# A long convolution's second stage split by halves of the channels, with a new written-out order

## The chip, the core and the metric

The kernel runs on one core of a Trainium2 chip. The metric is the device time of one execution in microseconds. The core has a matrix engine (TensorE, PE in the profile; PEld is its weight load), a vector engine (VectorE, DVE), a scalar engine (ScalarE, ACT), GpSimd (POOL), and SyncE (SP), which here only issues DMA transfers. Each engine works through its own queue in order; engines wait for one another on semaphores.

## What is computed

The input is a sequence of 2048 positions with 640 channels. A modulation vector from `c` and `w_mod` gives six vectors (sa, ca, ga, sb, cb, gb). The first half of the block is a long convolution, the second an MLP that shifts groups of channels along the sequence:

```python
mod = (_silu(c) @ w_mod).reshape(c.shape[0], 6, 1, -1)
h = _layernorm(x) * (1 + ca) + sa
# A: k_shift = four-tap convolution of k; kv = k_shift * v
kv_f, kf_f = rfft(kv padded to 4096), rfft(ssm_k padded to 4096)
y = irfft(kv_f * kf_f)[:2048] + kv * ssm_D
x = x + ga * (h * y)
h = _layernorm(x) * (1 + cb) + sb
# B: h1 = gelu(layernorm(h) @ w1), groups of it shifted by +-1, +-2; x1 = h + h1 @ w2
x = x + gb * (x1 + gelu(layernorm(x1) @ w3) @ w4)
```

## The kernel before

**The work.** The transforms are written as matrix products in two stages each, over 640 channels in five blocks (b0 to b4) of 128. The filter `ssm_k` (called s; `ssm_D` is added to its first column, L461) and kv go through the same forward transform:

- `to_slots` (L395): a 32x32 transpose on DVE for each block, 2048 columns.
- `stage1` (L408): for each block, half h of the positions inside it and quarter, four matmuls into PSUM, evacuated (L208 on ACT, L210 on DVE) as 128x1024 into `T01`, whose two halves `T0` and `T1` are the two values of h. One h holds 160 of the 320 values that the second stage has on its free axis.
- second stage: for each of 32 frequencies k, products of the table `Gs` (in `RG`) with `T01`, evacuated into `KSX` (buffer `R3`) for s and `XS` (buffer `R5`) for kv. For s this is `stage2` (L416): one frequency at a time over both halves, four matmuls of 320 columns and one evacuation of 128x640. For kv it is `stage2_half` (L434): one half at a time, three frequencies together, twelve matmuls of 160 columns and one evacuation of 128x960 (of 128x640 for the last two frequencies).

`inverse1` (L624 to L650) multiplies the spectra on DVE (L633, two products of 128x2048 for each of ten pieces, the second with a copy of s's piece whose partition halves are swapped by two DMAs, L629, into one of four buffers KSY), does the first inverse stage on PE (L644, L645) and evacuates into `T01`. `inverse2` (L673, L685) does the second. `k_shift` (L472) is the four-tap convolution on PE (L480) and the product with v on DVE (L485). Then for groups of tiles come `chain_a`, `chain_b`, `chain_c` (layer norms on DVE, ACT and POOL), `mm_w1`, `mm_w2`, `mm_w3`, `mm_w4`.

**Loads.** SP issues s's blocks (L229), the transposing loads of k and v (L234, one per block), copies that complete the table `Gs` (L354, L355), the input x (L540, in two sets of four), the twelve half loads of `w_mod` (L503; six early ones into `RH` and `RK`, six later ones into `R3`; each is used by five matmuls, L509), sixteen copies `RH<-RK` (L592), the KSY copies (L629) and the loads of w1 (L661), w2 (L662, L664), w3 and w4 (L1020 to L1023). POOL issues some of the copies.

**The order.** All work is added as numbered tasks. `ORDER` lists every task once: number, engine letter (P, A, D, G for POOL, S for SP) and for a PSUM tile its place, one of four. Each engine performs its tasks in the order of the list. The costs in `add` were used by the planner that wrote the list; at run time they do nothing.

Of the kernel before, what the change touches and what calls it, by code (L numbers as in the profile page):

```python
# [26 lines left out]
0S 2S 19G 18D 21G 20D 27G 29D 23D 4S 50G 28D 24A 36G 37G 22D 30A 68G 69D 25A 26G 88P:0 31A 89A 86P:1 87A 56G 90P:2 91A 72G 84P:3 5S 85A 3S 38G 39G 40A  # L27
73D 104P:0 106P:1 107A 70D 6S 49G 71D 105D 98P:2 102P:3 103A 99A 8S 118P:0 74G 94P:1 95A 75D 114P:3 115A 108P:2 109A 9S 119D 112P:0 113A 1S 66D 116P:1
41G 42G 43G 67D 80P:3 81A 117D 51D 52D 110P:2 44A 45D 10S 111D 96P:0 97A 82P:1 122P:3 11S 123D 32G 34G 54A 33S 53A 83A 76P:0 77A 100P:2 101D 92P:1 93A
78P:3 7S 120P:0 46G 136D 79A 55G 121D 175P:2 176A 47S 195P:1 196A 35S 179P:3 180A 185P:2 186D 147P:1 141P:0 193P:3 142D 148A 57G 58G 181P:2 182D 59G  # L30
139P:1 194A 140A 201S 199P:0 48S 200A 143P:3 144D 155P:2 165P:1 166D 156A 161P:0 162A 202S 191P:3 192D 12S 157P:2 158A 167P:1 168D 13S 163P:0 164A
197P:3 198A 145P:2 203S 146D 189P:1 65G 151P:0 152D 169P:3 190A 204S 183P:2 170A 184D 159P:1 160A 177P:0 178D 153P:3 154A 173P:2 174A 149P:1 150D
137P:0 260P:3 254D 171P:2 187P:1 138A 60A 188A 61G 62G 63G 261A 214D 172A 14S 124P:0 266P:1 210D 267A 125D 126P:3 127D 15S 211D 255D 209A 258P:2 259A
16S 270P:1 271A 130P:0 131D 268P:3 64A 262P:2 343G 269A 263A 215A 128P:1 264P:3 129D 256D 276P:2 277A 265A 134P:0 132P:1 17S 135D 282P:2 212A 283A
133D 216G 286P:3 223S 224P:0 220S 213G 278P:1 287D 225A 226S 279A 232S 284P:2 257D 221P:0 229S 285A 272P:3 227P:1 222A 228D 274P:2 235S 275D 273A
290P:0 291A 469D 288P:1 289A 233P:3 234D 292P:2 293A 294P:0 296P:3 230P:1 297A 298P:2 295D 299A 466D 342S 253G 246S 248G 312P:0 308P:3 309A 231D 463D
300P:1 301A 313D 460D 251G 310P:2 311D 367G 243S 306P:0 307A 316P:3 317D 280P:1 281A 252G 314P:2 304P:0 302P:3 305A 249S 240G 315D 236P:1 303A 237D
318P:2 319D 467D 340P:0 345D 241S 341A 338P:1 339A 238S 242G 326P:3 327A 344D 245S 250G 366S 322P:2 334P:0 352D 330P:1 331D 323A 244G 335A 239G 247G
324P:3 325A 346P:2 350S 351G 353D 347A 348P:0 360D 320P:3 349A 321A 328P:1 329A 354P:2 355A 359G 358S 361D 374S 356P:0 368D 369D 332P:3 333A 375G
362P:1 363A 364P:2 376D 365A 336P:3 337A 370P:1 371A 357A 372P:2 377D 378P:3 379A 380P:1 381A 383G 382S 385D 384D 386P:0 390S 391G 392D 393D 398S 373A  # L40
388P:3 387A 217A 399G 401D 394P:1 400D 425S 396P:2 397A 408D 407G 389A 402P:0 406S 409D 404P:2 395A 414S 416D 405A 415G 417D 464D 465D 426P:3 403A
427D 452S 410P:1 411A 412P:2 413A 420P:0 421D 418P:1 419A 422S 423P:3 456S 461D 470D 424D 468D 462D 218A 475P:20 477D 476A 520D 459G 454S 499D 500D
471D 521D 472A 540D 434S 219G 523D 541D 543D 437S 438P:1 439A 512A 435P:3 428S 429P:2 430A 431S 432P:0 501A 522A 433A 436A 525D 502G 504D 457S 478P:12
480A 503G 524G 526D 505D 473D 491P:03 545D 542A 544G 507D 553A 492A 527A 474D 546D 479A 571D 568D 485P:20 528G 529G 493A 530D 531P:1 506A 508G 509D
510P:3 486A 208S 547A 487A 458G 511A 548D 549G 481G 569D 570A 572D 573A 482P:20 484A 550D 551P:3 552A 532D 536P:1 533A 513D 537A 207S 574D 483D 575G
576D 580D 577D 517P:0 518A 581D 582D 583A 538P:3 578D 584G 579A 539A 585G 488P:21 489A 556P:0 557A 534D 535D 558P:3 559A 515P:2 516A 453S 514D 631D
632D 633A 586D 589D 590P:0 587P:3 455S 560P:2 634D 206S 635D 637G 591D 636A 638G 554D 561D 563D 588A 639D 562A 600P:0 601A 598P:3 599A 643D 640D 641D
642A 564G 494S 565D 644D 645D 646A 205S 441A 647D 490A 648G 566P:2 498G 567D 444D 651D 555D 605P:0 606D 607A 602P:3 649D 443D 603D 497S 652S 650S 699D
700D 447D 604A 620P:2 621A 495S 616P:1 617A 618P:0 661P:3 619A 662A 659P:2 660A 622P:1 623A 608D 609G 440D 610D 611P:0 613D 614P:3 615D 701A 663P:2
666P:1 664D 612A 683P:3 665A 667D 668A 681P:0 682A 677P:2 445G 656A 653D 654D 442G 655D 592D 669D 670G 674A 678A 671D 672P:1 673D 679P:0 680A 675P:1  # L50
593D 594D 702D 703D 496S 624P:2 595D 596D 676A 519G 597D 765D 749P:0 704A 705G 706G 766D 767A 768D 684A 707A 449A 625D 711D 747P:1 685P:32 712D 748A
769D 713D 714A 708D 709D 715D 771G 626D 446D 770A 710A 745P:1 716G 686P 717A 718S 772G 450D 719D 687D 720S 729P:3 773D 448G 750A 629S 774D 775D 777A
778D 779D 746A 727P:0 721D 781D 722D 723D 834D 835D 780A 776A 730A 627S 451G 790A 787A 657D 658D 782G 783D 743P:1 785D 791D 728A 731P:3 831D 832D 630S
688D 833A 732D 744A 733A 734P:0 735D 784S 786S 793P:1 794A 795P:3 737D 693D 694D 697S 736A 751P:02 796A 797P:1 800P:3 752P 738G 741D 836A 837G 838G
839D 753D 840D 798D 692S 739A 740S 742S 815P:0 843D 844D 801D 803D 841D 696S 813P:1 811P:3 845D 847G 842A 846A 848G 851D 788D 816A 849D 724A 725D 689S
809P:0 799A 852S 802A 804G 807D 814A 810A 812A 805D 850S 853P:1 759D 854A 808S 855P:2 856A 806S 875P:0 876A 869P:3 857P:1 873P:2 871P:0 726D 792D 874A
690S 789D 628S 754D 691S 891D 892D 894D 870A 860P:2 760D 951D 872A 895D 896A 695S 817P:30 893A 897G 898G 952D 954D 861D 862A 858D 863D 877P:21 953A
818P 903A 758S 904D 819D 899D 900D 698S 820D 859A 864G 865A 955G 905D 866S 906A 879D 822S 878P 867A 868S 933P:3 824S 901D 907G 902A 908G 909D 934A
911D 910S 956D 957D 958D 825D 912S 915P:2 935P:0 936A 913P:3 916A 763S 931P:0 757S 959A 914A 917P:2 929P:3 932A 960G 930A 961G 756S 821S 823S 962D
755S 963S 966P:0 967A 918D 919A 826D 885D 886D 920P:2 921D 830S 888S 829S 923G 762S 764S 922A 964P:1 965A 937P:30 969P:2 761S 880D 924G 968G 970D  # L60
972P:1 1003P:2 939D 925A 881S 1004D 926S 973D 975G 927A 928S 987P:3 988A 983P:2 971A 981P:1 890S 984A 1006G 974A 1005A 883S 889S 882S 827S 982A 985P:3
828S 976G 977D 1007G 938P 945D 979A 1008A 978S 980S 1010P:2 1011A 1012P:1 884S 1009S 946D 949S 1016P:0 1017A 948S 940D 942S 944S 1014P:2 943S 986A
989P:03 887S 1013A 1036P:1 991D 992D 996S 994S 1038P:0 990P 1015A 947S 997D 1034P:2 1039A 941S 1018P:03 1035A 1032P:2 1033A 998D 999S 1001S 993S 1002S
1042D 1043D 1000S 950S 1020D 1021D 1025S 1024S 1022S 1023S 1019P 1026D 1037A 995S 1027D 1031S 1029S 1030S 1028S 1040P:02 1044D 1045D 1047S 1046S 1048S
1049S 1041P 1050D 1051D 1052S 1053A 1054S 1055A
"""


# [69 lines left out]
def kernel(  # L138
# [4 lines left out]
    nc = tc.nc  # L143
# [11 lines left out]
    add = pl.add  # L155
# [444 lines left out]
    for h in range(2):  # L600
        stage2_half(h)
# [487 lines left out]
```

## Time and profile before

| what | value |
|---|---|
| median of 5 runs | 305.42 us (304.51 to 308.19) |
| the profiled execution | 308.19 us, its span 306.3 us, mean granted clock 0.965 |
| PE busy | 271.5 us (89%), 3054 matmuls |
| DVE, ACT, POOL busy | 218.1 us (71%), 210.2 us (69%), 112.2 us (37%) |
| stage 1, PE (L408) | 160 matmuls, 22.3 us |
| second stage of s, PE (L425) | 128 matmuls of 64x320, 11.2 us |
| second stage of kv, PE (L446) | 256 matmuls of 64x160, 10.4 us |
| evacuations of s's second stage | 20 on ACT (728 ns), 12 on DVE (819 ns) |
| products of spectra, DVE (L633) | 20, of some 1.22 us each |

The span runs from the first instruction to the last. Busy time counts what an engine's instructions cover; overlapping instructions make a busy PE no proof of a PE at its peak. "Idle before" in a group's line is the time in which the engine stood just before it, with what ended that wait.

### The profile page before, as it was taken

The page shows a single profiled execution, that of the slowest core. Times are in us where ns is not written, and L with a number is a line of the kernel's source. Part 1 is how long each engine was busy: PE and PEld are TensorE (multiplying, and loading weights), DVE is VectorE, ACT ScalarE, POOL GpSimd, SP SyncE. Part 2 cuts the span into 40 slices and gives each one's busy share as a digit, 9 for nine tenths or more (in the row PEclk, how much of TensorE's full clock was granted, in tenths as well). Part 3 has the DMA queues.
Part 4 walks back from the last instruction along what each step waited for, and adds up shares of the span by engine and source line. Part 5 has one row for each costly group of instructions (what it writes and reads, how often), then busy time and mean ns, then how long its engine had stood idle before and what let it go on. Part 6 is the DMA issues. An engine that isn't in the chain of part 4 may idle for free.

```text
span 306.3 us, 7652 instructions
## 1 busy us (share of the span) xinstructions
PE 271.5 (89%) x3054; PEld 207.1 (68%) x3054; DVE 218.1 (71%) x432; ACT 210.2 (69%) x352; POOL 112.2 (37%) x251
## 2 busy tenths in 40 slices
PE   0899999999889458687999989999999999999993
PEld 0655655777787236566887777688867886887771
DVE  8998999999899978869769986656475064031442
ACT  4789999999999699886768776276561752814110
POOL 4968553362104765341525660230152121400000
PEclk9999999999999855899999999999999999999999
DMA  6999999999899920642800112223004123130111
GB/s 216 261 191 202 221 205 162 262 234 209 202 226 303 244 49 2 204 144 46 288 3 1 24 39 55 54 43 77 2 18 86 28 55 70 26 86 5 32 51 43
DMA packets 58115, 35.75 MB, mean 117 GB/s; under 512 B 39872, under 2 KB 54848, under 8 KB 58080
## 3 DMA queue, kind: packets, MB, share of 16 engines
q1 hardware_dynamic: 56768, 31.55, 44.0%
q0 software_dynamic: 1216, 3.67, 4.9%
q8 instruction: 24, 0.39, 0.6%
q14 instruction: 11, 0.09, 0.1%
q10 hardware_dynamic: 96, 0.04, 0.1%
HBM read 16.31 MB, written 2.62 MB: 62 GB/s over the span
## 4 chain that ended last, share of the span: by engine, by line
PE 47%; DMA 15%; DVE 11%; SPq 7%; POOL 7%; issue 6%; ACT 6%; DVEq 0%; ACTq 0%; POOLq 0%
PE ps_w L931 17%; PE ps_w L961 15%; SPq L234 5%; PE ps_w L842 4%; PE ps_w L897 4%; DVE Rb L633 3%; DMA R<-in_A_v_dram 3%; DMA RG<-in_B_w_dram 3%; ACT RG L753 2%; POOL lnv L739 2%; DMA R<-RK 2%; DMA RH<-in_w_mod_dram 1%; DMA R<-in_w_mod_dram 1%; DMA RK<-R 1%; DVE Rb L395 1%
## 5 line engine op out<-in xcount | busy, mean ns | idle before, releaser
L931 PE MATMUL ps_w<-R,T 128*128 128x256 bf16 (+1 forms) x630 | 64.6, 261 | 1.1 <-DMA R<-RH 0.6
L931 PEld LDWEIGHTS <-T 128*128 128x128 bf16 x630 | 55.7, 98 | 8.7 <-issue 2.6
L935 ACT ACTIVATE R<-ps_w 128x1024 bf16<-128x1024 f32 (+2 forms) x36 | 29.0, 829 | 47.1 <-PE ps_w L931 47.0
L961 PE MATMUL ps_w<-T,R 128*128 128x320 bf16 x416 | 59.0, 299 | 0.0
L961 PEld LDWEIGHTS <-R 128*128 128x128 bf16 x416 | 40.2, 98 | 15.6 <-issue 0.5
L208 ACT CAST T<-ps_s 128x1024 bf16<-128x1024 f32 x34 | 32.7, 1027 | 3.6 <-PE ps_s L408 3.6
L753 ACT ACTIVATE RG<-R 128x640 bf16<-128x640 bf16 x32 | 23.6, 736 | 13.4 <-DVE R L780 9.0
L408 PE MATMUL ps_s<-F1bd,Rb 128*128 128x256 bf16 x160 | 22.3, 290 | 9.1 <-DVE Rb L395 8.8
L984 DVE TENSOR_TENSOR T<-ps_w,R 128x640 bf16<-128x640 f32 x15 | 12.3, 822 | 22.2 <-PE ps_w L952 11.5
L208 ACT CAST R<-ps_s 128x640 bf16<-128x640 f32 (+1 forms) x36 | 27.4, 845 | 0.9 <-PE ps_s L425 0.6
L408 PEld LDWEIGHTS <-Rb 128*128 128x128 bf16 x160 | 16.3, 104 | 15.1 <-DVE Rb L395 9.6
L897 PE MATMUL ps_w<-RG,R 128*128 128x320 bf16 x160 | 23.5, 300 | 0.0
L739 POOL TENSOR_TENSOR lnv<-lnv,mhalf 128x2 f32<-128x2 f32 (+1 forms) x29 | 22.5, 777 | 2.3
L842 PE MATMUL ps_w<-R,RG 128*128 128x256 bf16 (+1 forms) x200 | 21.2, 269 | 1.1 <-ACT Rb L208 0.5
L726 POOL TENSOR_SCALAR lnv<-stat 128x2 f32<-128x2 f32 (+1 forms) x14 | 5.4, 386 | 44.3 <-DVE Ra L764 17.2
L842 PEld LDWEIGHTS <-RG 128*128 128x128 bf16 x200 | 18.2, 108 | 3.3 <-issue 1.8
L904 DVE SCALAR_TENSOR_TENSOR R<-ps_w,R 128x640 bf16<-128x640 f32 x16 | 12.9, 819 | 10.6 <-PE ps_w L897 10.6
L644 PE MATMUL ps_i<-EA,Rb 128*128 128x128 bf16 x160 | 19.2, 219 | 1.0 <-DVE Rb L633 0.8
L645 PE MATMUL ps_i<-EB,Rb 128*128 128x128 bf16 x160 | 19.0, 219 | 1.3 <-DVE Rb L633 1.3
L897 PEld LDWEIGHTS <-R 128*128 128x128 bf16 x160 | 15.4, 98 | 6.1 <-issue 0.5
L480 PE MATMUL ps_ksh<-R,RQ 128*128 128x512 bf16 x80 | 18.8, 380 | 0.4 <-POOL RQ L356 0.4
L208 ACT CAST T<-ps_i 128x1024 bf16<-128x1024 f32 x19 | 18.2, 1046 | 0.9 <-PE ps_i L645 0.8
(179 smaller groups left out, 523.1 us busy)
## 6 DMA issues: line engine op xcount, KB each, us to landing
Ra<-in_A_ssm_k_dram SPq DMA_DIRECT2D x5, 512.0 KB, 5.1
Ra<-in_A_q_dram SPq DMA_DIRECT2D x8, 320.0 KB, 7.2
R<-in_w_mod_dram SPq DMA_DIRECT2D x6, 400.0 KB, 7.3
out_dram<-RH SPq DMA_DIRECT2D x60, 40.0 KB, 1.6
T<-in_B_w_dram SPq DMA_DIRECT2D x1, 2160.0 KB, 9.8
T<-in_B_w_dram SPq DMA_DIRECT2D x1, 2080.0 KB, 9.8
RH<-in_w_mod_dram SPq DMA_DIRECT2D x4, 400.0 KB, 5.9
RK<-R SPq DMA_DIRECT2D x5, 256.0 KB, 4.0
```

Source lines behind the costliest of these rows:

```text
L208: nc.scalar.copy(dst, src(ps.tile))
L408: nc.tensor.matmul(psv[:, ml, :], lhsT=xL[:, s0:s0 + P], rhs=F1r, start=True, stop=True)
L480: nc.tensor.matmul(pt[:, i, :], lhsT=diagw[:, b, jj, :], rhs=kT[:, b, c0:c0 + 512], start=(jj == 0), stop=(jj == 3))
L644: nc.tensor.matmul(psv[:, w, :], lhsT=Av[:, r_, :, g_], rhs=EAf, start=True, stop=False)
L645: nc.tensor.matmul(psv[:, w, :], lhsT=Bv[:, r_, :, g_], rhs=EBf, start=False, stop=True)
L739: nc.gpsimd.tensor_tensor(rs, rs, mhalf[:, 0:n], ALU.pow)
L753: add("ACT", 0.74, lambda e: nc.scalar.activation(junk, src, ACT.Square, scale=float(D) ** -0.5, accum_out=stat[:, li, 1, t:t + 1]), r=[sk ...
L842: nc.tensor.matmul(pt[:, fb, 0:cw], lhsT=w1_sb[:, b, 160 * fb:160 * fb + P], rhs=hT[:, b, 0:cw], start=(b == 0), stop=(b == ND - 1))
L897: nc.tensor.matmul(pt[:, hf, 0:320], lhsT=gsf[:, fb, c0:c0 + P], rhs=w2_sb[:, fb, 320 * hf:320 * hf + 320], start=(fb == 0), stop=(fb == 4))
L931: nc.tensor.matmul(pt[:, fl, 0:cw], lhsT=w3_sb[:, b, fb * P:(fb + 1) * P], rhs=xT[:, b, 0:cw], start=(b == 0), stop=(b == ND - 1))
L935: nc.scalar.activation(g3[g % 2][:, f0:f0 + fn, 0:cw], ps.tile[:, 0:fn, 0:cw], ACT.Gelu_apprx_tanh)
L961: nc.tensor.matmul(bank(i, hf), lhsT=gg[:, fb, i * P:(i + 1) * P], rhs=w4_sb[:, fb, 320 * hf:320 * hf + 320], start=(fb == 0 and i == 0), ...
```

## The change

Three edits. The function `stage2` goes; `stage2_half` takes the destination and its buffer as arguments and is called for s as well as for kv, so s too is done by halves of the channels, in threes of frequencies: 22 PE tasks and 22 evacuations in place of 32 and 32. The planner's cost of a PE task in it goes from 0.17 to 0.145 per frequency. `ORDER` is written anew for the 1036 tasks there now are (1056 before); task numbers above the second stage of s are lower by 20.

```diff
-    def stage2(XSd, dreg):
-        for k in range(32):
-            ps = Slot()
...
-                psv = pst(ps, name="ps_s2")[:, :, 0:320].rearrange("p g (h s) -> p g h s", h=2)
...
-    def stage2_half(h):
+    def stage2_half(XSd, dreg, h):
         for k0 in range(0, 32, 3):
             kn = min(3, 32 - k0)
...
-            t0 = add("PE", 0.17 * kn, f, r=[("T01", 10240 * h, 10240 * h + 10240), ("RG", 192 * k0, 192 * (k0 + kn))], alloc=ps, ni=8 * kn)
-            w = [("R5", 10240 * h, 10240 * h + 10240, "s2"), ("kT", 4 * h, 5, "s2")] + ([("vT", 0, 5, "s2")] if h else [("kTp", 0, 1, "s2")])
-            t1 = evac(XS[:, 160 * h:160 * h + 160, k0:k0 + kn, :],
+            t0 = add("PE", 0.145 * kn, f, r=[("T01", 10240 * h, 10240 * h + 10240), ("RG", 192 * k0, 192 * (k0 + kn))], alloc=ps, ni=8 * kn)
+            w = [(dreg, 10240 * h, 10240 * h + 10240, "s2")]
+            if dreg == "R5":
+                w += [("kT", 4 * h, 5, "s2")] + ([("vT", 0, 5, "s2")] if h else [("kTp", 0, 1, "s2")])
+            t1 = evac(XSd[:, 160 * h:160 * h + 160, k0:k0 + kn, :],
                       lambda t, kn=kn: t[:, :, 0:480].rearrange("p g (k s) -> p s k g", k=3)[:, :, 0:kn], 320 * kn, ps, w)
...
-    stage2(KSX, "R3")
+    for h in range(2):
+        stage2_half(KSX, "R3", h)
...
-        stage2_half(h)
+        stage2_half(XS, "R5", h)
```

What the new order does to the queues that matter here, told by name in place of the numbers:

| queue | before | after |
|---|---|---|
| SP, first loads | s b1, b3, b4, b2; k0, v0; s b0; k1, v1 | s b1, b3, b0, b4; k0, v0; k1; s b2; v1 |
| SP, up to the last v | table copies with c and one x load between, x, k2, v2, x, x, k3, v3, k4, v4 | three table copies, k2, two table copies, x four times, v2, k3, v3, k4, c, v4 |
| SP, early w_mod (numbered by use of the buffers 0 to 5) | 1, 0, 2, 4, 3, 5, then KSY of b0, six RH copies, KSY of b3, b1, b2, b4 | 1, 0, KSY of b0, 2, 3, 4, KSY of b3, three RH copies, 5, four RH copies, KSY of b1, b2, b4 |
| SP, after the last KSY copy | w1, one w_mod, two small w2 loads, four w_mod, one small w2 load, two x, w2, ... | one w_mod, w1, four w_mod, x, one small w2 load, w2, ... |
| PE, stage 1 and second stage of s | all twenty stage 1 tiles, then the second stage, frequency by frequency | the second stage of the first half begins with one stage 1 tile of the other half still to come; the two halves overlap, with kv's stage 1 and k_shift between them |
| DVE, start | transposes of s: b1, b3, b2, b4, k_shift of b0, b0 | b1, b3, b4, b0, k_shift of b0 twice, b2 |
| evacuations of s's second stage | 20 on ACT, 12 on DVE | 15 on ACT, 7 on DVE |
| ACT, second pass that makes the RH table | after all of ACT's share of s's second stage, with four of kv's stage 1 tiles and one ln1 statistic before it | with one tile of s's second stage still to come, five of kv's stage 1 tiles and two ln1 statistics before it |
| elsewhere | | some eighty tasks change engine: evacuations, norms, turns, layer-norm steps, small copies; the adds of `ssm_D` for b1, b3 and b4 go from POOL to DVE, the second sign table from DVE to POOL |

Buffers, the four places in PSUM and the arithmetic of every value stay as they are.

## The prediction

> **What bounds the kernel now.** I read the page first, then its busy slices, then a table of stretches, the timelines of ACT, DVE, PE and SP up to 130 us, the chain of work that ended last, and the waits. The stretches say that this is three kernels in a row:
>
> ```profile
> 28.00:40.00 12.00, 11.40 (x133) 6.80 (x130) 11.47 (x15) 11.64 (x19) 6.57 (x10) 1.00 1.12 221
> 40.00:54.00 14.00, 14.00 (x84) 7.95 (x83) 13.54 (x18) 13.91 (x24) 6.87 (x13) 1.00 1.11 180
> 98.00:108.00 10.00, 5.66 (x168) 3.35 (x172) 8.74 (x22) 6.91 (x15) 6.35 (x12) 0.81 1.12 257
> 146.00:180.00 34.00, 33.20 (x292) 26.59 (x291) 28.11 (x75) 25.15 (x49) 18.72 (x46) 1.00 0.27 78
> 250.00:302.00 52.00, 50.66 (x445) 38.63 (x442) 17.01 (x35) 16.70 (x27) 6.07 (x23) 1.00 0.20 47
> ```
>
> The columns are PE, PE weight loads, DVE, ACT and POOL busy, then the granted clock and the DMA share. Up to 98 us DVE and ACT, which empty PSUM, are both some 97% busy. From 146 us PE is never free for long: 153.2 of 156 us over the last four stretches. Between 98 and 146 us no engine is full; short chains of layer norms and late loads decide there. The edit lies in the first part; the new order touches all three. In the first part ACT and DVE run at these paces (start, length, engine):
>
> ```profile
> 29.54 10.18 ACT L208 CAST R<-ps_s 128x640 bf16<-128x640 f32 x16
> 29.79 9.45 DVE L210 CAST R<-ps_s 128x640 bf16<-128x640 f32 x12 [0.29 <-ACT R L208]
> 64.84 3.28 DVE L210 CAST R<-ps_s 128x960 bf16<-128x960 f32 x3
> 67.31 6.92 ACT L208 CAST R<-ps_s 128x960 bf16<-128x960 f32 x8
> 62.37 3.26 PE L446 MATMUL ps_s<-T,RG 64*128 64x160 bf16 x84
> ```
>
> The first two are the old second stage of s; the next three are the halved stage of kv, which has the shape that s is to get. Per instruction: ACT 10.18/16 = 0.636 and about 0.87 us, DVE 0.787 and 1.09 us, PE 39 ns. Two lines of the chain and the SP queue show the loads behind this stage:
>
> ```profile
> 43.57 9.17 DMA R<-in_A_v_dram
> 52.82 2.37 DVE R L485 x2
> ```
> ```profile
> 11.42 0.58 SPq L229 DMA_DIRECT2D Ra<-in_A_ssm_k_dram  x1
> 12.05 4.18 SPq L234 DMA_TRANSPOSE R<-in_A_k_dram  x1
> 26.59 0.46 SPq L355 DMA_DIRECT2D RG<-RG  x1
> 47.92 1.01 SPq L503 DMA_DIRECT2D RK<-in_w_mod_dram  x1
> 58.11 0.37 SPq L503 DMA_DIRECT2D RK<-in_w_mod_dram  x1
> 93.53 3.53 SPq L503 DMA_DIRECT2D R<-in_w_mod_dram  x4
> ```
>
> The last v block lands at 52.74; DVE had been idle for only 0.29 us. So loads and evacuation are level there, and a load that comes sooner is worth nothing unless ACT and DVE also have less to do.
>
> **The change, part by part.**
>
> *Evacuation of s's second stage.* Before: 20 on ACT and 12 on DVE, 20 x 0.636 + 12 x 0.787 = 12.7 + 9.4 us. After: by the new order 15 on ACT (one of 640 elements) and 7 on DVE (one of 640): 14 x 0.875 + 0.64 = 12.9 and 6 x 1.09 + 0.79 = 7.3 us. ACT +0.2, DVE -2.1.
>
> *Other work moved between the two up to the last inverse1 evacuation* (counted from both orders): ACT gets one stage1 evacuation (+0.95), loses one inverse1 evacuation (-0.94), one ln1 statistic (-1.72, from two passes and their reads) and has one table pass (-0.6) earlier, where it idled. Sum for ACT: -2.1 us. DVE loses one stage1 and gains one inverse1 evacuation (0), gains a statistic (+1.0), half a make_q (+0.45), three one-column adds of D (+0.4 at 0.13 each; +1.7 at the worst mean of 0.57) and loses the 0.29 us sign table, which goes to POOL at 1.5 us. DVE: -0.5 us. ACT ends this part (97.9 us), so ACT's -2.1 is what may reach the end; DVE's last product, 94.9 us now, stays ahead of it.
>
> *PE.* 128 matmuls of 320 columns become 256 of 160: 256 x 39 ns = 9.9 us. They lie under the evacuation of the same tiles, 20.2 us on two engines that also carry other work; I count 0. Without that cover all 9.9 us would be on the path. One rule speaks against this step: the Trainium skill, page "TensorE: Matmul & The Clock Gate", section on LDWEIGHTS, gives columns/1.2 ns for each weight load, 107 ns for 128 columns, whatever the other side is. As an estimate from that page 256 loads in series would take 27.3 us and make PE the bound of this stage by some 15 us. The trace has loads of 94 ns in this shape too, but they overlap: the spacing is 39 ns, and the row decides.
>
> *The s block b2* is loaded behind k1's transpose instead of ahead of it. SP's first loads end at 4.0 as now, k0 and v0 take 5.58 + 1.71, k1 4.18: the issue moves from 11.42 to about 15.6, and with a landing of 5.1 (median of the group) to 6 us the block is there at 21 to 22. DVE has by then done the other four blocks and both products of k0 by 18.7, so it stands 2.5 to 3 us, and the four stage1 tiles of b2 come late to ACT, which I make idle 1.4 + 0.8 us where it now idles 0.95 + 0.62 (its waits at 21.2 and 28.4). Cost on ACT: +0.7; ends 0 (if the block is early) and +2.
>
> *SP up to the last v.* k2 goes ahead of the wait for the table copies (26.59 now), all four x loads ahead of v2. From v1's end near 19: table copies 1.5, k2 3.15, copies 1.1, x 2.4, v2 2.2, k3 4.5, v3 2.9, k4 1.8, c 0.6: v4 is issued near 39 instead of 43.57 and lands near 48. DVE reaches that product near 49 by its own work. What it waited for goes; next late is ACT. Worth 0 by itself; its gain is the ACT sum above.
>
> *The w_mod loads of the first half.* The third (into RK) must wait until the table on ACT has been read out of RK; that pass moves back behind ACT's evacuations, from 46.65 to about 51 (ACT's counts at the paces above). Loads take from 4.56 (the chain's load at 56.97) to 7.5 us (median of this group), so its five matmuls come at 56 to 59.7, where PE's queue reaches them at 55.5. Behind them on PE stand seven stage1 tiles, behind its result on DVE two norms and three evacuations. ACT has tiles until 57.5: cost +0.3, ends 0 and +2.7. The sixth load (now 58.11) stands in SP behind a copy that waits for stage1 of b4 and three RH copies that wait for the fifth load's matmuls (about 61.9): it goes out near 63.5 and lands at 68 to 71.5. PE's queue reaches its matmuls at 68; behind them stand one stage1 tile and all of kv's second half, for which ACT waits. Cost +1.2, ends 0 and +3.5.
>
> *The w_mod loads of the second half* now stand ahead of the small w2 loads, for which SP waits 3.4 us:
>
> ```profile
> SPq L664 <- DVE Rb L633: 3.4, 1, 3.4
> ```
> ```profile
> PE ps_mod L509 <- DMA R<-in_w_mod_dram: 4.5, 4, 2.1
> ```
> ```profile
> 107.95 0.89 DVE L780 SCALAR_TENSOR_TENSOR R<-R,lnv,modv 128x640 bf16<-128x640 bf16 x1 [1.02 <-ACT modv L524]
> ```
>
> The four are issued from about 89 instead of 93.5; the last of them, used at 105.88 now, is there before 102. The idle of DVE falls away: -1.0; ends 0 (the DMA share is 0.97 in 90 to 98, the queue may simply be full) and -2.1 (PE's longest wait). Next late is the layer norm chain on POOL.
>
> *98 to 302 us.* Some forty norms, turns and layer-norm steps change engine. One pair of steps (0.92 + 0.61 on POOL at 111.6, on the chain) goes to DVE, where such steps take 0.15 + 0.21; another pair goes the other way. I count 0; ends -2.8 (all idle of PE after 146) and +3.0 (a gap as large as PE's 3.0 us between 130 and 146).
>
> **Sum.** -2.1 + 0.7 + 0.3 + 1.2 - 1.0 + 0 = -0.9 us, against the profiled execution: span 306.3 to 305.4, and 1.9 us around it, 308.19 to 307.3. That execution is the slowest of the five shown; their median is 2.8 us lower, so the median should go from 305.42 to 304.5.
>
> **Rivals.** *The front wins whole* (300.8): every wait of ACT before 98 us (88.7 us less 87.2 of work, 1.5) goes too: -2.1 - 1.5 - 1.0 = -4.6. For it: v4 lands 4 us sooner and halves let kv's first half start while s's second is still read. Against: b2's late block and PE's one queue. *PE held by late w_mod loads* (slower): the place is the third and sixth load of the first half, the price 2.7 + 3.5 in place of 0.3 + 1.2, so -0.9 + 4.7 = +3.8: 309.2. It decides from a sixth load that lands after about 70.5. For it: 7.5 us is that group's median. Against: the same loads have taken 4.56. By the page on TensorE above, section on the clock gate, a PE idle for over about 3.4 us also loses clock; the trace has 0.81 and 0.50 after its own gaps near 100 us, and 1.00 all through the first part. *A gap in the PE-bound part*: +3.0 on the forecast, 307.5. *The change does nothing* (305.4): ACT's saving is eaten by its waits; it lies inside the forecast.
>
> **How the numbers follow.** Forecast 304.5, chance 0.41, taken as within 1% (302.4 to 308.5, about what a measurement of this kernel can tell). Front whole 0.24, faster. Late w_mod loads 0.22, slower. PE gap 0.13, of which 0.05 within and 0.08 slower, as it ends close to the bound. So faster 0.24, same 0.46, slower 0.30. The range takes in the rivals of both signs, 300.8 to 309.2, with 0.3 and 0.8 beyond, since the gap can come on top: 300.5 to 310. The forecast's own range is 303 to 306.5.
>
> **What would show it.** Right: 15 and 7 evacuations of the s stage at 0.87 and 1.09 us; b2's transpose on DVE after 21 us with a wait on its load; last v before 50; no wait of PE on w_mod between 98 and 108. Wrong: waits of PE on RK's w_mod load over 2 us near 57 or 69; ACT's last inverse1 evacuation after 99 or before 95; a sum of PE idle after 146 that differs from 2.8 by over 2 us.

## The result and the profile after

The changed kernel takes 308.97 us (median; 307.37 to 312.88) against 306.81 us (304.12 to 310.18) for the kernel before, over all batches: ratio 1.0078 [1.0061, 1.0095], slower by 2.4 us by the ratio (2.2 by the two medians). The time lies in the outer range on record (300.5 to 310) and the ratio within 1%, but above the forecast's own range (303 to 306.5), and the sign of the forecast is wrong. The profiled execution took 310.64 us, span 308.8; forecast for it was 307.3.

Lines of code differ from those of before: evacuations are L207 (ACT) and L209 (DVE), stage 1 L407, the second stage L427, adds of `ssm_D` L444, `k_shift` L463 and L468, w_mod matmuls L493, products of spectra L617, first step of `chain_a` L745. The table of stretches of after, in the columns of before's table and with one stretch more:

```profile
28.00:40.00 12.00, 11.81 (x194) 8.20 (x192) 10.71 (x15) 11.90 (x16) 6.57 (x11) 1.00 1.08 189
40.00:54.00 14.00, 13.09 (x117) 6.85 (x116) 12.89 (x16) 11.99 (x20) 9.19 (x17) 1.00 1.08 210
54.00:70.00 16.00, 14.77 (x217) 11.31 (x213) 14.26 (x18) 14.01 (x18) 3.27 (x8) 1.00 0.80 185
98.00:108.00 10.00, 8.31 (x242) 6.10 (x240) 9.75 (x21) 9.42 (x18) 4.03 (x9) 1.00 1.12 268
146.00:180.00 34.00, 32.99 (x301) 26.44 (x297) 28.82 (x73) 25.76 (x51) 15.18 (x41) 1.00 0.32 82
250.00:302.00 52.00, 51.97 (x457) 40.33 (x454) 18.91 (x42) 16.31 (x28) 4.82 (x17) 1.00 0.18 42
```

And the line of before for the added stretch:

```profile
54.00:70.00 16.00, 15.58 (x239) 12.42 (x238) 15.11 (x20) 15.38 (x21) 8.18 (x17) 1.00 0.95 238
```

Read the fourth busy time of each line, that of ACT: 13.91 us of 14 before, 11.99 after; 15.38 of 16 before, 14.01 after. ACT, which ends the front part, lost 1.9 and 1.4 us of work done there (2.0 and 0.6 in e0, a second profile of the changed kernel). If it merely had less to do, the front would end sooner; it ends later:

| start or end (us, profiles) | before | after | after again (e0) | halved tiles in the old order (e5, e17) |
|---|---|---|---|---|
| last product of `k_shift` ends | 55.2 | 54.2 | 54.3 | 55.3, 55.1 |
| first product of spectra starts | 70.06 | 71.59 | 70.85 | 70.04, 70.89 |
| last inverse1 evacuation on ACT ends | 97.91 | 101.49 | 100.77 | 97.86, 97.91 |
| first step of `chain_a` starts | 100.54 | 104.25 | 103.64 | 100.49, 100.54 |
| from there to the span's end | 205.8 | 204.55 | 202.4 | 202.0, 204.7 |

So 3.1 to 3.7 us are lost by 100 us, and no loss shows after; single profiles of one kernel differ by 2 to 3 us in the last row, so what is won or lost there can't be read. The last column belongs to two runs of the experiments, the same tiles in the old order. Busy times up to the last inverse1 evacuation, in the columns of the tables above (before, after, and e5):

```profile
0.00:97.91 97.91, 84.88 (x984) 61.13 (x985) 92.66 (x124) 88.39 (x119) 48.84 (x84) 1.00 0.97 221
0.00:101.49 101.49, 85.62 (x1112) 62.65 (x1113) 94.19 (x125) 88.05 (x110) 48.81 (x78) 1.00 0.98 219
0.00:97.86 97.86, 84.15 (x1108) 63.90 (x1113) 91.85 (x120) 88.11 (x113) 48.77 (x84) 1.00 0.95 221
```

ACT's busy time is 88.4 us before and 88.0 after: its work fell by 0.4 us, its idle time rose from 9.5 to 13.4 us (12.8 in e0). In e5 ACT has the same 88.1 us of work and stands only 9.8 us. Where it stood, in ACT's timeline of after (from two windows):

```profile
41.88 0.96 ACT L207 CAST R<-ps_s 128x960 bf16<-128x960 f32 x1 [0.63 <-PE ps_s L427]
...
50.73 0.99 ACT L207 CAST R<-ps_s 128x960 bf16<-128x960 f32 x1 [0.78 <-PE ps_s L427]
...
58.83 4.70 ACT L207 CAST T<-ps_s 128x1024 bf16<-128x1024 f32 x5
64.96 1.84 ACT L207 CAST R<-ps_s 128x960 bf16<-128x960 f32 x2 [1.43 <-PE ps_s L427]
...
73.92 5.07 ACT L207 CAST R<-ps_s 128x640 bf16<-128x640 f32 x6 [0.54 <-PE ps_s L427]
```

In before, and once more in e0, the wait ahead of kv's second stage (64.96 above) is shorter:

```profile
63.00 3.55 ACT L208 CAST R<-ps_s 128x960 bf16<-128x960 f32 x4 [0.25 <-PE ps_s L446]
```
```profile
64.23 1.84 ACT L207 CAST R<-ps_s 128x960 bf16<-128x960 f32 x2 [0.63 <-PE ps_s L427]
```

Each bracket names PE. PE's own timeline says what it stood for at the largest of them, and the chain that ended last has the same load:

```profile
59.08 3.39 PE L407 MATMUL ps_s<-F1bd,Rb 128*128 128x256 bf16 x28
63.54 0.85 PE L493 MATMUL ps_mod<-RH,silu_w 128*128 128x320 bf16 x5 [1.07 <-DMA RH<-in_w_mod_dram]
64.33 1.70 PE L427 MATMUL ps_s<-T,RG 64*128 64x160 bf16 x44
...
70.92 0.84 PE L493 MATMUL ps_mod<-RK,silu_w 128*128 128x320 bf16 x5
```
```profile
30.20 7.05 SPq L233
...
43.18 5.03 DMA R<-in_A_k_dram
...
58.28 5.22 DMA RH<-in_w_mod_dram
```

The fifth early w_mod load goes into a buffer that the second one's matmuls free at 58.25; it is issued at 58.28 and used at 63.54. kv's second stage stands behind it in PE's queue, so ACT waits too. In e0 PE waits 0.40 us for this load in place of 1.07. The sixth (70.92) is used without a wait, though its issue came late, as SP's timeline shows along with the loads of v:

```profile
27.16 3.00 SPq L524 DMA_DIRECT2D Ra<-in_A_q_dram  x4
30.20 7.05 SPq L233 DMA_TRANSPOSE R<-in_A_v_dram  x1
...
46.80 2.43 SPq L233 DMA_TRANSPOSE R<-in_A_v_dram  x1
...
56.73 1.92 SPq L487 DMA_DIRECT2D RH<-in_w_mod_dram  x2
...
66.37 0.53 SPq L487 DMA_DIRECT2D RK<-in_w_mod_dram  x1
```

v2's issue behind the four loads of x took 7.05 us (5.55 in e0, 2.19 before), and the last v went out at 46.80 (44.05 in e0), not near 39 (43.57 before). `k_shift` ends at the same time in both profiles of the changed kernel, though the last v differs by 2.75 us.

### The profile page after: what moved, and what is told of

Same layout as the page of the kernel before. It is cut to its first block, busy times and chain, and to the rows that moved or that the text cites. A ratio compares the mean times of both kernels' runs of the same rounds, so it can differ in the third digit from the quotient of the medians.

```text
span 308.8 us, 7891 instructions
## 1 busy us (share of the span) xinstructions
PE 273.6 (89%) x3182; PEld 209.8 (68%) x3182; DVE 220.8 (72%) x435; ACT 210.3 (68%) x346; POOL 108.1 (35%) x242
## 4 chain that ended last, share of the span: by engine, by line
PE 48%; DVE 21%; ACT 10%; DMA 7%; SPq 5%; POOL 4%; issue 3%; POOLq 0%; ACTq 0%; DVEq 0%
PE ps_w L945 14%; PE ps_w L915 13%; PE ps_w L881 5%; SPq L233 4%; ACT RG L737 3%; ACT T L207 3%; DVE R L764 3%; DVE Rb L394 3%; PE ps_s L427 3%; POOL lnv L723 3%; PE ps_w L826 2%; PE ps_ksh L463 2%; DVE Ra L748 2%; DMA Ra<-in_A_ssm_k_dram 2%; PE ps_s L407 2%
## 5 line engine op out<-in xcount | busy, mean ns | idle before, releaser
L207 ACT CAST T<-ps_s 128x1024 bf16<-128x1024 f32 x35 | 34.0, 1031 | 3.1 <-PE ps_s L407 3.0
L407 PE MATMUL ps_s<-F1bd,Rb 128*128 128x256 bf16 x160 | 23.3, 291 | 10.2 <-DVE Rb L394 10.0
L207 ACT CAST R<-ps_s 128x960 bf16<-128x960 f32 (+1 forms) x31 | 28.3, 962 | 4.1 <-PE ps_s L427 3.9
L407 PEld LDWEIGHTS <-Rb 128*128 128x128 bf16 x160 | 15.8, 104 | 16.4 <-DVE Rb L394 10.7
L974 DVE TENSOR_TENSOR RH<-T,Ra 128x640 bf16<-128x640 bf16 x15 | 7.4, 492 | 27.1 <-DMA out_dram<-RH 23.1
L881 PE MATMUL ps_w<-RG,R 128*128 128x320 bf16 x160 | 24.8, 310 | 0.4 <-ACT R L828 0.4
L427 PE MATMUL ps_s<-T,RG 64*128 64x160 bf16 x512 | 21.7, 230 | 2.1 <-ACT T L207 1.2
L427 PEld LDWEIGHTS <-RG 64*128 64x128 bf16 x512 | 17.6, 94 | 6.9 <-issue 6.4
L723 POOL TENSOR_TENSOR lnv<-lnv,mhalf 128x2 f32<-128x2 f32 (+1 forms) x29 | 20.6, 711 | 2.3
L463 PE MATMUL ps_ksh<-R,RQ 128*128 128x512 bf16 x80 | 18.8, 380 | 0.4 <-DMA R<-in_A_k_dram 0.3
```

The source lines that it names most:

```text
L207: nc.scalar.copy(dst, src(ps.tile))
L407: nc.tensor.matmul(psv[:, ml, :], lhsT=xL[:, s0:s0 + P], rhs=F1r, start=True, stop=True)
L427: nc.tensor.matmul(psv[:, g, j], lhsT=Gs[p, k, 64 - 64 * cc:192 - 64 * cc], rhs=T1h[h][p, cc * 32 + k], start=(cc == 0), stop=(cc == 1), t ...
L463: nc.tensor.matmul(pt[:, i, :], lhsT=diagw[:, b, jj, :], rhs=kT[:, b, c0:c0 + 512], start=(jj == 0), stop=(jj == 3))
L723: nc.gpsimd.tensor_tensor(rs, rs, mhalf[:, 0:n], ALU.pow)
L881: nc.tensor.matmul(pt[:, hf, 0:320], lhsT=gsf[:, fb, c0:c0 + P], rhs=w2_sb[:, fb, 320 * hf:320 * hf + 320], start=(fb == 0), stop=(fb == 4))
```

## The experiments

Two theories stood at the start: the new order, or a load in it, takes time from ACT in the front; or (rival B) the halved form itself costs time. A third, rival C, puts the cost into the new order behind 100 us. Ratios are to the kernel before, with 95% intervals; 0.0033 is 1 us, and a point is 0.01, some 3.1 us. A task is written as its number and engine letter.

### The form and the order apart

**e1_form_only**: before's order, with s's second stage in the new form.

```diff
-    stage2(KSX, "R3")            # 32 pairs of tasks
+    for h in range(2):
+        stage2_half(KSX, "R3", h)  # 22 pairs, spread over the old positions
```

> Halved second stage of s (22 tiles in threes, 14 evacuations on ACT and 8 on DVE), everything else in the order of before. Theory A (the loss of 2.2 us is made by the new order of the first 100 us, not by the form of the tiles): ACT 13 x 0.87 + 0.64 = 12.0 in place of 12.7 us, DVE 7 x 1.09 + 0.79 = 8.4 in place of 9.4, so 0 to 1.0 us below before, about 306.3. Rival B (the form itself costs, through 256 weight loads in place of 128): as slow as after, 308.5 to 309.5.

Measured: 1.0057 [1.0027, 1.0088]. Slower than before, so the form looks guilty; but its stretch of 30 to 40 us, and PE in it, show another cause:

```profile
30.00:40.00 10.00, 7.56 (x185) 6.33 (x181) 7.61 (x8) 7.35 (x9) 4.68 (x9) 1.00 1.13 215
```
```profile
34.39 1.01 PE L427 MATMUL ps_s<-T,RG 64*128 64x160 bf16 x24 [0.43 <-ACT R L207]
```

Three engines are each some 75% busy: PE waits for an evacuation to free a place in PSUM, and the evacuators for PE. The tiles had inherited the places of the old, smaller ones.

**e5_form_places** and its repeat **e17_form_places_again**: e1 with the PSUM places given in turn from the first tile of s's second stage to its last, nothing else. 22 places differ; seven of them belong to tiles of kv's stage 1 and of `k_shift` that stand between.

```diff
-153P:3 157P:2 155P:0 139P:3 145P:0 143P:2 141P:1 147P:2
+153P:1 157P:3 155P:2 139P:0 145P:3 143P:0 141P:2 147P:1
...
```

> As the run with the form alone (halved tiles in the order of before), but the PSUM places from the first tile of the second stage of s to its end are given in turn, so that no tile needs a place that was taken two tiles ago. In the first run ACT stood 2.65 us and DVE 2.4 us between 30 and 40 us, each behind a tile that waited for its place. If that was only the places: these waits go (ACT over 9.5 of 10 us there), the time falls by 1.5 to 2.5 us against the first run, to 306 to 307.3, level with before or just under it (the evacuations save 0.7 us of ACT and 1.0 of DVE). If the form itself costs (rival B): it stays at 1.005 of before.

> The run with halved tiles, places in turn and the old order, once more. If the halved form is worth what its evacuations save: 0.994 to 1.000 of before again. If the first value was a lucky one: 1.003 to 1.006, as with the poor places.

Measured: 0.9976 [0.994, 1.0011] and 0.9992 [0.9967, 1.0017]. The same stretch of e5:

```profile
30.00:40.00 10.00, 9.37 (x218) 7.93 (x214) 9.11 (x9) 9.52 (x13) 4.71 (x10) 1.00 1.14 198
```

The places alone are worth 0.65 to 0.8 points, 2 to 2.5 us. "Perfetto Trace Analysis" of the Trainium skill, section "Matmuls", asks for independent matmul groups to go through different PSUM banks in rotation, so that evacuation and matmuls overlap; e1 against e5 agrees: PE's waits for an evacuation between 28 and 70 us fall from 3.2 to 1.5 us (1.4 in e17). With places in turn the form is level with before: rival B falls, and the 0.8 to 1.0 points between e5 or e17 and after are those of the order. The order's own places weren't varied; PE's waits for an evacuation in the same stretch are 0.5 us in after and 0.2 in e0, so they can't make up much of the loss.

**e0_after_again**: the changed kernel once more, beside e5's batch mates, as a measure of spread.

> The changed kernel as it is, beside the three that follow, on the same chip: 0.6 to 1.0% slower than before; the base from which the others are counted.

Measured: 1.0067 [1.0032, 1.0102]; the front's landmarks stand in the table above.

**e2_front_old, e3_front_new, e11_form_new_rest**: one part of the order from each side, cut where inverse1 ends.

```diff
 e2:  ORDER = front of e1 + rest of after
 e3:  ORDER = front of after + rest of before
 e11: ORDER = front of e5 + rest of after
```

> The first kernel's work up to the last inverse1 evacuation (order of before, halved form), and everything behind it in the order of after. Theory A: the front ends about where it ended before (98 us), and the new order behind it is worth the 1 us that after wins back between 104 and 302 us: about 305.5. Rival C (the new order behind 100 us is what costs): about 309. Theory B: 308 or more.

> Work up to the last inverse1 evacuation in the order of after, everything behind it in the order of before. Theory A: the front ends 3.5 us late, as in after, and nothing wins it back: about 310. Rival C: about 306.5, since the old order behind 100 us returns.

> The halved form with its places in turn and the old order up to the last inverse1 evacuation (305.4 us when whole in the old order), and behind it the order of after. If the new order behind 98 us is neutral, as the equal 166.1 us from the first w3 matmul to the end in before and after say: 304.5 to 306.5. If it costs: 307.5 or more. If it wins the 1 us by which the gap of after shrinks behind 104 us: under 304.5.

Measured: 1.0117 [1.0085, 1.015], 1.0135 [1.01, 1.0171], 1.0094 [1.0061, 1.0128]. e3 is slower than both whole orders of which it is made, e2 and e11 are so by less than their intervals: a seam has a cost of its own. Rival C alone is out, for e3 has the old order behind the front and is no faster. But theory A gave e2 305.5 and the neutral reading gave e11 304.5 to 306.5; at 310.6 and 309.3 both missed, as if the new order behind the front cost time too. In e2 ACT stands at it for 1.55 us, where neither before nor after has a wait of ACT at this evacuation (in e11 it is 2.61, and 3.05 at ACT's next one):

```profile
103.96 0.96 ACT L207 CAST Rb<-ps_i 128x960 bf16<-128x960 f32 x1 [1.55 <-PE ps_i L669]
```

These hybrids can't apportion the loss between front and rest. The landmarks put it into the front; that the rest is neutral isn't shown, since its length differs by 2 to 3 us between profiles of one kernel.

### The w_mod loads

**e4_loads_in_turn**: after, with the loads asked for sooner without a new buffer.

```diff
-PE: kv stage 1, kv stage 1, 204P (second w_mod)   SP: 209S (fourth), 212S (fifth)
+PE: 204P, kv stage 1, kv stage 1                  SP: 212S, 209S
```

> After, with two moves: the five matmuls of the second early w_mod load stand two stage 1 tiles earlier in PE's queue (they free the buffer of the fifth load, which is issued at 58.28 in after), and the fifth load is issued ahead of the fourth. Theory A1 (inside A: this load, on which PE waits until 63.5 us, is one of the front's two losses): PE's wait of 1.07 us for it goes, ACT's wait of 1.43 at 65 shrinks to under 0.5, the last inverse1 evacuation comes 0.7 to 1.1 us earlier, about 308.3. Rival (that wait is covered by what stands behind it): within 0.2 us of after, 309.0.

Measured: 1.0139 [1.0106, 1.0172], slower than after, which neither side had forecast. The fifth load's waits went, but PE stood for the sixth instead, and ACT for the stage 1 tiles that were pushed back (1.47 us at 58.77):

```profile
72.13 0.85 PE L493 MATMUL ps_mod<-RK,silu_w 128*128 128x320 bf16 x5 [1.26 <-DMA RK<-in_w_mod_dram]
```

**e7_kv_halves**: after, with two halved kv tiles ahead of the fifth load's matmuls, the sixth load ahead of the copies for b3, and the last two stage 1 tiles earlier.

```diff
-213P 294P 298P ... 284P 288P ... 268P ... 266P     SP: 212S ... copies, 215S, 346S
+294P 298P 213P ... 268P 266P 284P 288P             SP: 212S, 215S, 346S ... copies
```

> After, with kv's second stage reordered: the matmuls of the fifth early w_mod load (PE waits for it until 63.5 us) stand behind the first two tiles of kv's first half and not ahead of them; the sixth load is issued ahead of the copies for b3 and RH; the last two stage 1 tiles stand two tiles earlier on PE and one evacuation earlier on ACT. Theory A3 (the rest of the front's loss is ACT standing 1.43 us at 65 behind that load and 0.83 at 69 to 74 behind the last stage 1 tiles): these waits shrink from 2.3 to under 0.7, the time falls by 1.0 to 1.6 us against after. Rival (one wait is traded for another, as when the loads were put in turn): within 0.4 us of after.

Measured: 1.0137 [1.0094, 1.018], slower than after and outside both forecasts. New waits came in: PE on DVE's evacuation of a w_mod product (1.07 us) and on a product of spectra (1.25), then ACT on PE:

```profile
79.41 0.96 ACT L207 CAST R<-ps_s 128x960 bf16<-128x960 f32 x1 [1.89 <-PE ps_s L427]
```

**e8_own_buffer**: after, with the fifth load in a piece of `modv` that isn't used yet, issued ahead of the fourth.

```diff
+    wx = (modv[:, 2:5, :].rearrange("p j d -> p (j d)")[:, 0:1600]..., ("modB", 0, 100))
-        w, wk = wm[i % 3] if i < EARLY else wl[i - EARLY]
+        w, wk = wx if i == 4 else wm[i % 3] if i < EARLY else wl[i - EARLY]
-SP: 209S 212S
+SP: 212S 209S
```

> After, with the fifth early w_mod load given a buffer of its own (a part of modv that is not written before the second half), so that it no longer waits for the second load's matmuls, and issued ahead of the fourth; no other queue is changed. Theory A3 (ACT's wait of 1.4 us near 65, behind PE's wait for this load, is part of the loss): the load is issued near 54 in place of 58.3, PE's wait of 0.4 to 1.1 us and ACT's of 1.2 to 1.4 go, the time falls by 0.8 to 1.2 us against after. Rival (another wait takes its place, as in the two runs that moved queue entries): within 0.4 us of after.

Measured: 1.0039 [1.0005, 1.0072], the only edit of after that came out faster: 0.28 to 0.39 points, 0.9 to 1.2 us, against 1.0067 and 1.0078, though the intervals overlap. ACT's timeline of e8 (its lines are one higher) has no wait where after has 1.43 us:

```profile
58.70 4.70 ACT L208 CAST T<-ps_s 128x1024 bf16<-128x1024 f32 x5
63.52 1.84 ACT L208 CAST R<-ps_s 128x960 bf16<-128x960 f32 x2
```

So the wait at this load goes, 0.6 us (e0) to 1.4 (after). How much of it reaches the end isn't settled: the last inverse1 evacuation ends at 100.54, 0.2 us sooner than in e0 and 0.95 sooner than in after, for ACT then stands 0.83 us behind PE at 98.6 (0.24 in e0). About 1 us of the loss is this load's buffer, by an estimate from the times that isn't clear of their noise.

**e15_form_own_buffer**: the like edit in e5, for its sixth load, ahead of the fourth and fifth.

```diff
-        w, wk = wm[i % 3] if i < EARLY else wl[i - EARLY]
+        w, wk = wx if i == 5 else wm[i % 3] if i < EARLY else wl[i - EARLY]
-SP: 212S ... 215S
+SP: 215S 212S
```

> The old order with halved tiles and places in turn, and the sixth early w_mod load in a buffer of its own, issued ahead of the fourth and fifth. DVE stands 0.4 us near 68 behind its product; that goes. 0.2 to 0.5 us under the run with halved tiles alone, about 0.996 of before. If that load is not what DVE waits for: level with it.

Measured: 1.0032 [0.9992, 1.0071]; no gain on 0.9976 and 0.9992, where 0.996 was expected. Another load of the group is late instead:

```profile
62.90 0.85 PE L494 MATMUL ps_mod<-RH,silu_w 128*128 128x320 bf16 x5 [1.25 <-DMA RH<-in_w_mod_dram]
```

### The stretch of 40 to 54 us

Theory **A2**: k and v come late here because x's four loads go ahead of v2. Rival **P**: PE's queue holds ACT, since `k_shift`'s matmuls stand between s's halved tiles.

**e6_x_last** and **e10_x_last_silu**: after, x's loads behind the last v; the statistics that read x moved behind. e10 also moves POOL's silu forward.

```diff
-SP: 183S 181S 184S 182S, v2, k3, v3, k4, c, v4
+SP: v2, k3, v3, k4, c, v4, 183S 181S 184S 182S
-DVE: 189D 191D 190D 194D and ACT: 192A 195A at 38 to 50 us
+both behind k_shift
+POOL: 65G ahead of 193G        # e10 alone
```

> After, with the four x loads moved from ahead of v2 to behind v4 on SP, and the first six layer-norm statistics of x moved behind them on DVE and ACT. Theory A2 (part of the front's loss is that the k and v blocks stand behind x: k4 lands at 48.2 and PE waits for it): v4 is issued near 43 in place of 49.2, ACT's four waits of 1.94 us in all between 40 and 54 us shrink below 0.7, the time falls by 1.0 to 1.6 us against after. Rival (the transfers share one bandwidth and ACT, DVE and PE are near full there anyway): within 0.4 us of after, or slower by what the late statistics cost.

> The run with the x loads behind v4 once more, with POOL's silu step ahead of the layer-norm step, so that the first w_mod product does not stand 5.9 us behind POOL. In the first form PE was full from 34 to 56 us and k_shift still ended at 54.1, though k4 and v4 had landed some 6 us sooner. If that reading holds (PE's own queue sets this stretch, not the loads): within 0.6 us of after. Theory A2 (the late k and v blocks cost): 1.0 to 1.6 us faster than after.

Measured: 1.0342 [1.0291, 1.0393] and 1.0195 [1.0156, 1.0234]. In e6 PE stood for POOL, which had the silu behind a step that waited for the moved statistics:

```profile
62.77 1.51 PE L493 MATMUL ps_mod<-RH,silu_w 128*128 128x320 bf16 x5 [5.92 <-POOL silu_w L386]
```

e10 is free of that. Its last v was issued at 38.90, 5 to 8 us sooner than in e0 and after, and yet `k_shift` ended at 54.3, as in after, for now PE was full and DVE and ACT stood:

```profile
40.00:54.00 14.00, 13.89 (x130) 7.60 (x131) 10.75 (x8) 10.44 (x15) 7.14 (x10) 1.00 1.06 210
```

Late loads alone don't make the end of `k_shift`: A2 falls on this landmark. The time of e10, 1.2 points above after and outside both forecasts, says nothing on it: its fourth and fifth w_mod loads go out 2.6 us later than in after and its sixth 3.7, PE waits 2.5 us for the last two, and the front ends at 105.9.

**e12_after_two_taps** and **e13_form_two_taps**: two of the four taps left out in after and in e5 (`k_shift` then isn't the full convolution), so PE has half of that work.

```diff
-                for jj in range(4):
+                for jj in range(2):
-... stop=(jj == 3))
+... stop=(jj == 1))
```

> After, with only two of the four taps in k_shift's matmuls (the convolution of k leaves out two taps): ten PE tiles of 1.75 us become 0.87, nothing else changes. Theory P (between 40 and 62 us PE's queue sets the pace in after): ACT's waits of 1.9 us between 40 and 54 fall under 0.7, the last k_shift product ends before 52 in place of 54.2, and the time falls by 1.5 to 2.5 us against after, to 0.998 to 1.002 of before. Rival E (ACT and DVE set it, as the prediction had it): within 0.7 us of after.

> The same two taps left out in the old order with halved tiles and places in turn (305.4 us whole). There ACT is 98% busy from 40 to 70 us, so theory P expects 0.8 us at most: 0.994 to 0.998 of before. If PE is worth the same in both orders, the fall equals that of the run before.

Measured: 1.0147 [1.0094, 1.0201] and 0.9989 [0.9954, 1.0025]. e13 is level with e5 and e17: in the old order the lighter PE is worth nothing. e12 is slower than after by 0.7 points. In e12 PE is light, ACT has 0.9 us more done, and `k_shift` ends at 55.3, later than in after:

```profile
40.00:54.00 14.00, 8.75 (x89) 4.86 (x89) 11.43 (x14) 12.91 (x20) 9.71 (x17) 1.00 1.02 206
```
```profile
47.70 1.04 PE L463 MATMUL ps_ksh<-R,RQ 128*128 128x512 bf16 x4 [1.15 <-DMA R<-in_A_k_dram]
...
54.20 0.59 PE L427 MATMUL ps_s<-T,RG 64*128 64x160 bf16 x12 [2.37 <-DVE R L468]
```
```profile
52.92 2.36 DVE L468 TENSOR_TENSOR R<-ps_ksh,R 128x1024 bf16<-128x1024 f32 x2 [1.88 <-issue]
```

PE waits for k, then for DVE's last product. For DVE's 1.88 us the profile names nobody; the matmuls were done, and the last v, issued at 46.27, would be there at 52.5 by the 6.2 us that such loads take in this stretch, so the load is the likeliest. P falls as the only cause as well. Why e12 ends its front at 103.1, later than after with less work on PE, isn't explained; its loads were late too (k0's issue took 7.45 us, 6.91 in after and 6.30 in e0).

**e16_x_last_two_taps**: both at once (e10 with two taps; the same part is left out).

```diff
 e10, and
-                for jj in range(4):
+                for jj in range(2):
```

> After with both: x loads behind v4 (silu ahead on POOL) and two of four taps left out of k_shift's matmuls. If the last v block and PE's queue are two limits at nearly the same time (v4 lands at 52.7, PE is full to 54), only both together move the stretch: the last k_shift product ends before 51, and the time falls by 2 us or more against the run with x last alone (312.5). If a third limit stands at 54 us, it ends there again and the time stays within 1 us of that run.

Measured: 1.0162 [1.0126, 1.0198]. Only with both lifted does `k_shift` end sooner, at 48.4; then x is late:

```profile
46.10 2.34 DVE L468 TENSOR_TENSOR R<-ps_ksh,R 128x1024 bf16<-128x1024 f32 x2
51.68 0.89 DVE L538 BATCH_NORM_STATS2 ln_st<-Ra 128x6 f32<-128x320 bf16 x2 [3.23 <-DMA Ra<-in_A_q_dram]
```

For the end of `k_shift`, then, PE's queue and the loads of k and v are two limits close together: lifting one alone gains nothing, lifting both gains 5.9 us. It doesn't reach the end: the time is 0.7 us under e10's, where 2 or more were forecast, and the front ends at 103.3, as x is now late.

### Two smaller suspects

**e9_early_b2**: after, b2 of s loaded ahead of k1 again, and three adds of `ssm_D` on POOL.

```diff
-SP: 10S (k1), 3S (b2)     DVE: 72D 74D 66D
+SP: 3S, 10S               POOL: 72G 74G 66G ahead of 49G
```

> After, with block b2 of s loaded ahead of k1's transpose as in before, and the adds of D for b3, b4 and b0 on POOL ahead of its long step at 10 us (on DVE one of them took 1.9 us there). Theory A4 (PE is the full engine from 20 to 62 us in after, and what it lost between 10 and 20 us, 1.1 us against before, is never won back): PE busy over 9.2 of 10 us between 10 and 20, the time falls by 0.8 to 1.2 us against after. Rival (PE then only waits longer for k4, which lands at 48.2): within 0.4 us of after.

Measured: 1.0105 [1.0059, 1.015], no gain. PE's share of 10 to 20 us was 8.44 of 10 (8.37 in after), under what I had set as the condition for a verdict, since POOL's adds came late:

```profile
10.55 3.98 DVE L394 STREAM_TRANSPOSE Rb<-Ra 128x1024 int32<-128x1024 int32 x2 [2.18 <-POOL Ra L444]
```

So it decides nothing on b2.

**e14_stat_on_act**: after, one statistic of layer norm from DVE to ACT near 50 us.

```diff
-194D
+194A
```

> After, with one layer-norm statistic of x put back from DVE (1.05 us) to ACT (1.72 us) near 50 us, where ACT stands 0.8 us. Theory P: ACT has the time, since PE is late; within 0.5 us of after. Rival E (ACT ends this part and every microsecond of its work reaches the end, the working behind the -2.1 us of the prediction): 1.2 to 1.7 us slower than after.

Measured: 1.0143 [1.0096, 1.019]. By the time alone this is rival E's forecast, 1.4 us more than after. By the profile it isn't: ACT took the statistic in time in which it had waited, and the last inverse1 evacuation (100.72) and `chain_a` (103.59) stand as in e0. So one profile says that ACT isn't short of time near 50 us; why the kernel is still 0.65 points slower than after stays open.

## Why the prediction was wrong

**The step that failed is "ACT's -2.1 is what may reach the end".** It held ACT to be the bound of the front and took PE and the loads as covered. Two parts of that were off. ACT's work fell by 0.4 us, not 2.1 (0.6 of which was a table pass moved into idle time, no work saved): the groups of ACT have, the first line (kv's tiles) in before up to 97.91 us and the others in after up to 101.4,

```profile
L208 ACT CAST R<-ps_s 128x960 bf16<-128x960 f32 x15 | 13.9, 1008 | 0.2 <-PE ps_s L446 0.2
...
L207 ACT CAST R<-ps_s 128x960 bf16<-128x960 f32 x29 | 27.0, 981 | 3.3 <-PE ps_s L427 3.1
L207 ACT CAST T<-ps_i 128x1024 bf16<-128x1024 f32 x18 | 17.1, 1036 | 0.5 <-PE ps_i L629 0.3
```

and the step's terms came out as below. And the front ended later, not sooner: ACT's idle time grew by 3.3 (e0) to 3.9 us, of which 2.6 to 3.3 lies between 36 and 72 us. e5 has the same tiles and the same work of ACT without these waits, so the new order makes them. The experiments name two places where ACT isn't what sets the pace: up to 54 us PE's queue with the loads of k and v, near 64 the fifth w_mod load. The 97% of ACT and DVE in before (from 28 us on) were no proof that PE and the loads had slack.

| term | forecast | measured |
|---|---|---|
| ACT: s's evacuations, stage 1, inverse1, statistic, table | +0.2, +0.95, -0.94, -1.72, -0.6 | +0.9, +1.3, -1.1, -1.6, 0 |
| ACT's work, and its end | -2.1, -2.1 | -0.4, +3.6 (+2.9 in e0) |
| b2: ACT's waits at the start | +0.7 | waits 2.5 in place of 1.8; idle up to 40 us 8.3 in place of 7.9 |
| SP to the last v | issue near 39, worth 0 | issue 46.80 (44.05 in e0); sooner loads alone don't end `k_shift` sooner (e10) |
| third w_mod load | +0.3 | a wait of 0.49 on DVE |
| fifth w_mod load | not priced | ACT's wait 1.43 (0.63 in e0); about +1 by e8, within noise |
| sixth w_mod load | +1.2, issue near 63.5 | 0; issue 66.37, used at 70.92 without a wait; 1.26 in e4 |
| second-half w_mod loads | -1.0 | from the last inverse1 evacuation to `chain_a` 2.76, was 2.63: 0 |
| 98 to 302 us | 0 | 0: idle of PE after 146 3.4 by the stretches, was 2.8 |
| sum | -0.9 | +2.45 between the profiles, +2.4 by the ratio |

Point by point. **Evacuation**: 15 and 7 as counted; 0.875 us for a 960-wide one came from one row of eight; all fifteen of kv in before took 13.9 us, 0.93 each, and here it is 0.92 to 0.93. **DVE**: forecast -0.5 with +0.4 to +1.7 for three adds of D; the five adds took 2.9 us on DVE, one of them 1.97 (last section), against 1.1 for two before, so this term came out at its worst case. **PE, costed at 0**: the spacing of 39 ns held, and e5 shows the halved form to be level. But the cover that I named, evacuation, was gone in 40 to 54 us: with two taps out ACT did 0.9 us more there. So PE isn't hidden there; it is a limit beside the loads (e12, e16). **b2**: the transpose starts at 22.05, as forecast after 21, though DVE had waited for PE's `k_shift` and not for the load; its cost in the end wasn't isolated (e9). **SP**: I took v2's issue at 2.2 us as it was; behind four x loads it is 7.05, and with k0 (6.91, was 5.58) at the start that is 6.2 of the 7.8 us between 39 and 46.8. **Second-half loads**: PE's waits for them between 98 and 146 us fell from 4.3 to 1.2 us, as forecast, but PE then stood 4.3 us for an ACT evacuation, and nothing was gained. **Fifth load**: I followed the third and the sixth into `RK`, since they were moved, and not the fifth, which stands on the same rule one buffer on: freed by 204P's matmuls, a landing of 5.2 us, PE's whole kv half behind it.

**The rivals.** *PE held by late w_mod loads* (309.2 forecast, 309.0 measured) had the right kind, but the wrong loads: the fifth, not the third and sixth, and it makes about 1 us of the loss and not 4.7. That its time was nearly right is luck. *The front wins whole* is refuted by 101.49; its 1.5 us of waits was misread too, for ACT is busy 85.2 of those 88.7 us, so they were 3.5. *A gap in the PE-bound part*: no, 3.4 us of idle in all from 146 us. *The change does nothing* is what the form alone does (e5, e17). My own sign of being wrong, "ACT's last inverse1 evacuation after 99", is the one that came.

**What stays open.** Of some 2.6 to 3.1 us between after and the same tiles in the old order, e8 accounts for about 1, within noise. The rest, 1.5 to 2 us, lies in the front by the landmarks, with 1.9 us of waits of ACT in 40 to 54 us; no single limit was found behind them, as e6, e10, e12 and e16 lifted one each, or both, and met the next, and no edit of the written order alone (e4, e7, e9, e14) came out faster than after. Between 36 and 72 us PE is idle 2.2 us in after and 2.4 in e0, against 1.3 in e5 and 1.7 in e17; ACT is idle 4.0 and 3.3, against 0.5 and 1.3. So PE stands about a microsecond more and ACT 2 to 3.5; what PE does first may matter more than how long it stands, but that isn't shown, and which tasks would have to move together isn't settled. No version here is clearly faster than before; e5 and e17 are level with it and 0.8 to 1.0 points faster than after.

## What to carry to other kernels

Work taken from an engine that is 97% busy is worth something only if what stands next to it has slack: check the queue of PE and the landing of each load in that stretch before booking a saving, and follow every load of a buffer ring, the unmoved ones too, from the matmul that frees the buffer to the one that waits. When tile sizes change, give the PSUM places anew; inherited ones cost 2 to 2.5 us here and looked like a cost of the new form. Orders cut and joined at a seam, or a planned order edited at one point, showed new waits at the joint here (e2, e4, e7), which hid what was to be measured.

## What the runs showed of the hardware

**A one-column add that takes 1.97 us.** Three of the five adds of D on DVE took 0.15 to 0.23 us in after. Two took longer, in DVE's timeline and POOL's:

```profile
8.39 0.45 DVE L444 TENSOR_TENSOR Ra<-Ra,Dcol 128x1 bf16<-128x1 bf16 x1
...
10.84 2.04 DVE L444 TENSOR_TENSOR Ra<-Ra,Dcol 128x1 bf16<-128x1 bf16 x2
```
```profile
7.56 1.27 POOL L310 TENSOR_TENSOR R<-R 128x512 f32<-128x512 f32 x1
...
10.33 2.46 POOL L355 TENSOR_SCALAR_AFFINE_SELECT RQ<-skT 128x2560 bf16<-128x2560 bf16 x1
```

The first ends at 8.84, POOL's step at 8.83; the second group begins with the add of 1.97 us, which ends at 12.81, and POOL's long step ends at 12.79. "SBUF — State Buffer" of the Trainium skill, section "Who interferes with whom", has a rule that fits: a DVE instruction with two inputs in SBUF and a GpSimd instruction that reads SBUF exclude each other, and the one that comes second is blocked until the first is done. Both rows agree with it.

**The issue of a transposing load isn't a constant.** v2's took 2.19 us on SP before and 7.05 in after, behind four x loads; k0's 5.58 and 6.91, behind the first loads in another order. The same order with the x loads behind the last v (e10) has v2 at

```profile
26.30 3.83 SPq L233 DMA_TRANSPOSE R<-in_A_v_dram  x1
```

and e6 and e16, built the same way, at 3.27 and 3.45; with x ahead it took 5.55 to 7.05 us (e0, e12, after). So what stands ahead of a transposing load changes its price here, by some 2 to 4 us, and executions of one order still differ by 1.5 us. How it does so no run shows.
